# A frequency filter and a two-layer network: one product bank shared by two engines, later requests of x, four PSUM banks at first, and another queue for a split store

## The chip, the cores and the metric

The kernel runs on one core of a Trainium2 chip. The core has a matrix engine (TensorE, "PE" in the profile, with its weight loads as "PEld"), a vector engine (VectorE, "DVE"), an activation engine (ScalarE, "ACT"), GpSimd ("POOL") and SyncE ("SP"), which here only issues DMAs. Each engine works through its own instructions in order and waits on semaphores for the others. TensorE's results go to PSUM, which has eight banks of 512 floats per partition.

The metric is the device time of one execution in microseconds. The kernel before took 750.02 us (median of 14 runs, 749.25 to 751.09).

## The reference

```python
def _attn_ref(x, filt_r, filt_i):            # x: 8 x 3008 x 256
    X = np.fft.rfft(x, axis=1)
    F = (filt_r + 1j * filt_i)[None, :, :]
    return np.fft.irfft(X * F, n=x.shape[1], axis=1).astype(np.float32)

def _moe_ref(x, w_in, w_out):                # x: 24064 x 256, d_ff 2048
    h = x @ w_in
    g = np.maximum(0.01 * h, h)
    return (g @ w_out).astype(np.float32)
```

The output of the first is the input of the second; all inputs and the output are float32 in HBM.

## The kernel before

The Fourier transform over 3,008 points is split as 94 by 32. For each of the 8 batches there are four matmul stages: s1 (over 94 points), s2 (over 32), a product with the filter, sa (back over 32) and sb (back over 94), which leaves the mixed batch transposed in `yt`, in fp16. The network then takes the 24,064 rows in 47 chunks of 512: `moe1` multiplies `yt` by `w_in` into one of two double PSUM banks (`ph`, L505) and ScalarE applies the leaky ReLU into `gt_c` (L510); later chunks' second layer uses a seven-product scheme (L569), the first three chunks a plain one (L630).

All instructions are placed by hand or by a planner; each engine then runs its own list in that order.

**The first batch** is written out as a list of steps, the string `FIRST` (L461 to L478). Its five banks are b0 to b2 (single, `pf`) and b3, b4 (double, `ph`, 1,024 floats each). The steps that matter here:

- `s2p hf c n i b` fills bank b with stage s2 for n frequencies from c on, for channel half hf; i is 0 or 1 for the two terms of the complex product (L392, L396).
- `s2d` lets VectorE multiply such a bank by the filter into `prods` (L400). `s2a` lets ScalarE copy four frequencies of a bank to a spare in SBUF (L410), and `s2m` lets Pool multiply that spare by the filter (L400 too, on POOL).
- `sap hf c b` is stage sa for four frequencies (L420); it reads both products, i = 0 and 1. `sae` is ScalarE's copy of the result to `big2` (L423). `t2` is a VectorE transpose (L429); two of the four read channel half 0, two half 1. `sbp` is stage sb (L437) and `sbe` its copy to `yt` by ScalarE or VectorE (L336). `warm` are matmuls on idle data.
- `x 0`, `x 1` and `w_out` are DMA requests on Pool's queue: the two halves of the second batch's x (L191) and `w_out` (L456).

In `FIRST`, bank b4 holds s2 for half 1, frequencies 8 to 15, term 1 (`s2p 1 8 8 1 b4`); VectorE multiplies all of it (`s2d 1 8 8 1`). The bank is filled again by `s2p 1 0 8 0 b4`. On Pool the order is: six products, `x 0`, `s2m 1 16 8 0`, `s2m 1 16 8 1`, `x 1`, `w_out`.

**After the first batch** work is placed by planned times: `at(time, f)` puts f on a heap, and times are in units of which a chunk has `SL = 8`. The stages of the second batch (`s1_group`, L249 to L259, with their matmul at L254 and the copy at L257) run between the matmuls of the first chunks. Their banks come from `bank("pf", ...)` (L154), which goes round the list `single`. At the end of the first batch `single.pop()` (L489) leaves two banks in it; the third, `psp_last`, and `po_ps` become the output banks of the second layer, which uses them from time 8 on. `late_sb` (L446) places the rest of the first batch's stage sb among this work, from the same two banks.

**The stores.** A chunk's rows are stored in four blocks of 128 rows; `stores(ci, i)` issues blocks 2i and 2i + 1. A block that crosses a multiple of 376 rows is split into two requests. In the last chunk, i = 1 is stored first and i = 0 last, and block 1 (i = 0, j = 1) is a split one. All stores go out on SyncE's queue but for the last chunk's blocks with j = 1, which go out on ScalarE's (L584).

Of the kernel before, what the change touches and what calls it, by code (L numbers as in the profile page):

```python
# [75 lines left out]
def kernel(  # L76
# [9 lines left out]
    nc = tc.nc  # L86
    B, N, D = x.shape
# [6 lines left out]
    NCHUNK = TOK // CH  # L94
    assert NCHUNK * CH == TOK
    SL = 8
# [52 lines left out]
    single = [psp.tile([P, CH], FP32, name=f"pf{i}") for i in range(3)]  # L149
    po_ps = psp.tile([P, 2, D], FP32, name="po_ps")  # L150
    psp_last = single[-1]
# [12 lines left out]
    def at(time, f):  # L164
        clock["n"] += 1
        heapq.heappush(work, (time, clock["n"], f))
# [185 lines left out]
    act, dve = nc.scalar.copy, nc.vector.tensor_copy  # L352
# [6 lines left out]
    held, spare = {}, [scrp.tile([P, 4, DH], FP32, tag=f"p{i // 2 + 1}", name=f"spare{i}") for i in range(6)]  # L359
# [39 lines left out]
    def times_filter(eng, hf, c, n, i, x):  # L399
        eng.tensor_tensor(prods[hf][:, i, ds(c, n), :], x, fa_sb[:, ds(c, n), ts(hf, DH)], AL.mult)  # L400

    def s2d(hf, c, n, i):
        times_filter(nc.vector, hf, c, n, i, held.pop(("s2", hf, c, i)))

    def s2a(hf, c, n, i):

        at_c = c if ("s2", hf, c, i) in held else c - 4
        held["xf", hf, c, i] = xf = spare.pop(0)
        key = ("s2", hf, at_c, i)
        act(xf[:], (held.pop(key) if c - at_c == n - 4 else held[key])[:, ds(c - at_c, 4), :])  # L410

    def s2m(hf, c, n, i):
        xf = held.pop(("xf", hf, c, i))
# [44 lines left out]
    def round_x(n0, n, e):  # L458
# [10 lines left out]
        s2a 1 16 8 0, s2p 0 4 4 0 b1, s2p 1 16 8 1 b3, s2d 0 4 4 0, s2a 1 20 8 0, sap 0 8 b2, s2d 0 4 4 1,  # L469
        s2a 1 16 8 1, s2a 1 20 8 1, s2m 0 12 4 0, s2p 0 16 8 1 b4, sap 0 0 b1, s2p 1 0 8 1 b3, s2m 0 12 4 1,  # L470
        sap 0 12 b0, s2m 1 20 8 0, sae 0 8 A, s2d 0 16 8 1, sae 0 0 A, s2p 1 8 8 1 b4, sap 0 4 b2, s2d 1 0 8 1,
        sap 0 16 b1, sae 0 12 A, s2p 1 8 8 0 b3, sap 0 20 b0, s2d 1 8 8 1, s2m 1 20 8 1, sae 0 4 A,
        s2d 1 8 8 0, s2p 1 0 8 0 b4, sae 0 16 A, sap 1 20 b2, s2d 1 0 8 0, sap 1 12 b1, sae 0 20 A, sap 1 8 b0,
        x 0, s2m 1 16 8 0, sae 1 20 A, s2m 1 16 8 1, x 1, w_out, sae 1 12 A, sae 1 8 A, sap 1 16 b3,
        sae 1 16 A, sap 1 4 b2, t2 1, sae 1 4 A, sap 1 0 b4, t2 0, sae 1 0 A, warm 4, sbp 0 1 b1, sbp 0 4 b0,
        sbp 0 0 b3, sbp 0 3 b2, t2 3, sbe 0 1 A, sbe 0 4 A, sbe 0 0 A, sbp 0 2 b4, sbp 0 7 b1, sbp 0 6 b0,
        t2 2, sbe 0 2 A, sbe 0 7 A, sbp 0 5 b3, sbp 1 0 b4, sbp 1 1 b1, sbe 0 6 A, sbe 0 5 A, sbe 1 1 A,
        sbe 0 3 D, sbe 1 0 D  # L478
    """
    steps = dict(s1p=s1p, s1e=s1e, t1=t1, s2p=s2p, s2d=s2d, s2a=s2a, s2m=s2m, sap=sap, sae=sae, t2=t2,  # L480
                 sbp=sbp, sbe=sbe, x=load_x, w_out=load_w_out, xc=round_x, warm=keep_warm)
    for step in FIRST.split(","):
        what, *args = step.split()
# [5 lines left out]
    single.pop()  # L489
    out_banks = [t[:].rearrange("p (a t d) -> p a t d", a=2, t=2)  # L490
                 for t in (psp_last, po_ps.rearrange("p a d -> p (a d)"))]

    gts, osts, phs = {}, {}, {}

# [26 lines left out]
    s1, s2, s4 = (sums[:, i] for i in range(3))  # L521
# [26 lines left out]
    def store(ci, tj, of, queue=nc.sync):  # L548

        t, end = ci * CH + tj * P, ci * CH + (tj + 1) * P  # L550
        lo = 0
        while t < end:
            e = min(end, (t // QT + 1) * QT)
            b, h = divmod(t // QT, N2 // 4)
            row = b * N + (t % QT) // 4 * N2 + 4 * h
            queue.dma_start(
                bass.AP(tensor=out.tensor, offset=out.offset + row * D,
                        ap=[[N2 * D, (e - t) // 4], [D, 4], [1, D]]), of[lo : lo + e - t])
            lo, t = lo + e - t, e
# [15 lines left out]
    def rows(ci, i):  # L575

        if (ci, i) not in osts:
            osts[ci, i] = outp.tile([P, 2, 3, P], FP32, tag="ost", name=f"ost_c{ci}_h{i}")
        return osts[ci, i]

    def stores(ci, i, of=range(2)):
        for j in of:
            store(ci, 2 * i + j, rows(ci, i)[:, j, 0:2, :].rearrange("p k d -> p (k d)"),
                  nc.scalar if ci == NCHUNK - 1 and j else nc.sync)  # L584

    def twice(po):
        ap = [list(v) for v in po.ap]
# [4 lines left out]
    def last_product(ci):  # L592
        def after(po):
            add(rows(ci, 0)[:, :, 1], po, rows(ci, 1)[:, :, 2], AL.add)
            soon(AFTER[5], lambda: stores(ci, 0))
        return product(ci, lambda: sum_places(ci)[3], b22, after, 3)

    def products(ci):
        a11, a12, a21, a22 = (lambda i=i, j=j: quarter(ci, i, j) for i in range(2) for j in range(2))

        def after5(po):
            add(rows(ci, 1)[:, :, 1:3], twice(po), part[1], AL.add)
            soon(AFTER[5], lambda: stores(ci, 1))

        def m1():
            return product(ci, a11, b11, lambda po: nc.scalar.copy(t1, po))

        def m2():
            return product(ci, a12, b21, lambda po: add(rows(ci, 0)[:, :, 0], po, t1, AL.add))

        def m7():
            return product(ci, lambda: sum_places(ci)[1], wt[2], lambda po: add(v7, po, t1, AL.add), 1)

        if ci == NCHUNK - 1:
            items = last_product(ci - 1) + m1() + m7() + m2()
        elif ci > W0:
            items = m1() + last_product(ci - 1) + m2() + m7()
        else:
            done["products"] += 1
            items = m1() + [lambda: None] * (2 * NCH) + m2() + m7()  # L620
        items += product(ci, lambda: sum_places(ci)[2], wt[1], lambda po: add(part[1], twice(po), part[0], AL.add), 2)
        items += product(ci, a22, wt[3], lambda po: add(rows(ci, 1)[:, :, 0], po, u3, AL.add))
        items += product(ci, lambda: sum_places(ci)[0], wt[0], after5, 0)
        return items + last_product(ci) if ci == NCHUNK - 1 else items
# [44 lines left out]
    for b in range(1, B):  # L669
        z = 47 * (b - 4) if b > 4 else 0  # L670
        p = PLANS[min(b, 4) - 1]
# [18 lines left out]
    while queue:  # L690
        time, n, stage, b, g, f = heapq.heappop(queue)
# [62 lines left out]
```

## Time and profile before

| | |
|---|---|
| time, median of 14 runs | 750.02 us |
| the profiled execution, its time | 750.27 us |
| its span, first to last instruction | 748.5 us |
| ScalarE busy | 559.5 us, 75% |
| VectorE busy | 501.1 us, 67% |
| Pool busy | 164.1 us, 22% |
| first matmul of `moe1` (L505) | starts at 34.47 us |
| last vector result of the last chunk (L594) | starts at 742.84 us, takes 0.42 |

The span is what the trace covers; the execution's own time has 1.8 us around it. The profile's rows give start and length in us, the engine, the source line, and what the instruction writes and reads, then how many instructions are merged in the row; in brackets stands the idle time of the engine before it and the instruction that ended it. A queue that only issues DMAs has a q behind the engine's name. Matmuls overlap each other in the pipeline: a row of two matmuls of 0.38 us each that is 0.59 long has starts 0.21 apart. TensorE's granted clock is full in this run but for the last microseconds.

### The profile page before, as it was taken

How to read it: one execution, taken by the hardware profiler on the slowest of the kernel's cores; microseconds unless marked ns; L12 is line 12 of the kernel's file. 1: busy time of each engine (PE TensorE's matmuls, PEld its weight loads, DVE VectorE, ACT ScalarE, POOL GpSimd, SP SyncE). 2: the span in 40 equal slices, each digit the busy share in tenths (PEclk: the TensorE clock that was granted, in tenths of full speed). 3: DMA queues.
4: the chain of work that ended last, by engine and by line, in shares of the span. 5: the costliest groups of instructions: out<-in, count | busy, mean ns of one | idle time of the engine just before them, and what ended most of it. 6: DMA issues, size and time to landing. Idle time of an engine off the chain costs nothing.

```text
span 748.5 us, 19408 instructions
## 1 busy us (share of the span) xinstructions
PE 738.6 (99%) x8017; PEld 529.0 (71%) x8017; DVE 501.1 (67%) x684; ACT 559.5 (75%) x755; POOL 164.1 (22%) x171
## 2 busy tenths in 40 slices
PE   9999999999999999999999999999999999999996
PEld 3556667777687777877778777777777777777775
DVE  5987646766676765766777667766676675565565
ACT  4776797888778787777777787787777777777662
POOL 5603422332232212121232222121212210000000
PEclk9999999999999999999999999999999999999999
DMA  9997798887876666755675656544454333111111
GB/s 205 228 222 189 187 222 219 203 208 197 202 191 156 151 184 184 169 134 165 192 179 149 158 160 172 158 133 111 143 165 120 97 107 107 50 55 54 33 52 59
DMA packets 119560, 113.64 MB, mean 152 GB/s; under 512 B 16352, under 2 KB 92768, under 8 KB 119280
## 3 DMA queue, kind: packets, MB, share of 16 engines
q1 hardware_dynamic: 104127, 94.66, 42.7%
q0 software_dynamic: 15056, 17.49, 16.1%
q8 instruction: 62, 1.02, 0.6%
q10 hardware_dynamic: 289, 0.26, 0.1%
q14 instruction: 26, 0.21, 0.1%
HBM read 57.51 MB, written 50.33 MB: 144 GB/s over the span
## 4 chain that ended last, share of the span: by engine, by line
PE 93%; DMA 3%; DVE 2%; ACT 1%; issue 1%; POOL 0%; SPq 0%; DVEq 0%; POOLq 0%; ACTq 0%
PE ph L505 42%; PE po_ps L569 18%; PE pf L569 17%; PE pf L254 3%; PE pf L346 3%; PE pf L303 2%; PE pf L325 2%; DMA p_b_g<-p_b_g 2%; PE po_ps L368 1%; PE pf L630 1%; PE po_ps L630 1%; DMA dz<-big 1%; DMA big<-dz 0%; POOL y_b_g L318 0%; ACT yt L336 0%
## 5 line engine op out<-in xcount | busy, mean ns | idle before, releaser
L510 ACT ACTIVATE gt_c<-ph 128x1024 f16<-128x1024 f32 x376 | 385.6, 1026 | 134.8 <-PE ph L505 124.1
L505 PE MATMUL ph<-yt,w_in_sb 128*128 128x512 f16 (+7 forms) x1728 | 447.3, 351 | 0.2 <-ACT yt L336 0.2
L569 PEld LDWEIGHTS <-gt_c 128*128 128x128 f16 x2800 | 202.2, 98 | 91.2 <-issue 0.2
L318 POOL TENSOR_TENSOR y_b_g<-p_b_g,p_b_g 128x512 f16<-128x512 f32 x84 | 114.2, 1360 | 418.4 <-DMA p_b_g<-p_b_g 239.3
L569 PEld LDWEIGHTS <-big 128*128 128x128 f16 x2128 | 151.3, 98 | 61.6 <-issue 0.2
L505 PEld LDWEIGHTS <-w_in_sb 128*128 128x128 f16 x1728 | 137.5, 98 | 20.3 <-issue 0.7
L312 DVE TENSOR_TENSOR p_b_g<-pf,fb_sb 128x512 f32<-128x512 f32 x78 | 53.6, 688 | 32.4 <-PE pf L303 19.8
L569 PE MATMUL po_ps<-wt_sb,gt_c 128*128 128x128 f16 x704 | 70.0, 219 | 0.0
L569 PE MATMUL pf<-wt_sb,gt_c 128*128 128x128 f16 x688 | 68.4, 219 | 0.0
L569 PE MATMUL pf<-w_out_sb,gt_c 128*128 128x128 f16 x720 | 67.9, 219 | 0.0
L569 PE MATMUL po_ps<-wt_sb,big 128*128 128x128 f16 x720 | 67.4, 219 | 0.0
L569 PE MATMUL pf<-wt_sb,big 128*128 128x128 f16 x704 | 67.2, 219 | 0.0
L257 ACT CAST big<-pf 128x512 f16<-128x512 f32 x100 | 58.2, 587 | 11.9 <-PE pf L254 10.5
L569 PE MATMUL po_ps<-w_out_sb,gt_c 128*128 128x128 f16 x688 | 66.0, 219 | 0.0
L336 ACT CAST yt<-pf 128x376 f16<-128x376 f32 x120 | 56.4, 472 | 10.8 <-PE pf L346 7.9
L542 DVE TENSOR_TENSOR big<-gt_c 128x2048 f16<-128x2048 f16 (+1 forms) x46 | 57.9, 1259 | 0.1
L315 DVE TENSOR_TENSOR p_b_g<-pf,fa_sb 128x512 f32<-128x512 f32 x84 | 57.2, 681 | 0.2
L542 DVE TENSOR_TENSOR gt_c<-gt_c 128x2048 f16<-128x2048 f16 x43 | 55.4, 1288 | 1.0
L542 DVE TENSOR_TENSOR big<-gt_c,big 128x2048 f16<-128x2048 f16 (+1 forms) x45 | 55.2, 1227 | 0.0
L542 DVE TENSOR_TENSOR big<-big,gt_c 128x2048 f16<-128x2048 f16 (+1 forms) x45 | 54.6, 1212 | 0.1
L327 ACT CAST big<-pf 128x512 f16<-128x512 f32 x84 | 49.0, 584 | 4.9 <-PE pf L325 3.0
L254 PE MATMUL pf<-x_sb,small_sb 94*128 94x512 f16 x112 | 42.7, 381 | 0.6 <-ACT big L257 0.6
(88 smaller groups left out, 621.4 us busy)
## 6 DMA issues: line engine op xcount, KB each, us to landing
dz<-big SPq DMA_DIRECT2D x98, 256.0 KB
p_b_g<-p_b_g SPq DMA_DIRECT2D x156, 128.0 KB
out_dram<-ost_c_h SPq DMA_DIRECT2D x119, 128.0 KB
big<-dz SPq DMA_DIRECT2D x42, 256.0 KB
big<-dz SPq DMA_DIRECT2D x56, 192.0 KB
x_sb<-in_x_dram POOLq DMA_DIRECT2D x40, 192.0 KB, 4.8
x_sb<-in_x_dram POOLq DMA_DIRECT2D x2, 768.0 KB, 9.3
w_in_sb<-in_moe_w_in_dram POOLq DMA_DIRECT2D x1, 1024.0 KB, 13.5
```

Source lines behind the costliest of these rows:

```text
L254: nc.tensor.matmul(ps, fwd1[:N1], x_sb[:N1, ds(2 * g, 2), :], start=True, stop=True)
L257: copy(st[:, ds(2 * (g % 2), 2), :], ps)
L312: nc.vector.tensor_tensor(p2[:], ps, fb, AL.mult)
L315: nc.vector.tensor_tensor(p1[:], ps, fa, AL.mult)
L318: ("y", b, g), lambda: nc.gpsimd.tensor_tensor(y1[:], p1[:], p3[:], AL.add)))
L327: nc.scalar.copy(st2[h % 4][:, ds(2 * (g % 2), 2), :], ps)
L336: copy(yv, ps.rearrange("p c a -> p a c"))
L346: nc.tensor.matmul(ps[:, j, :], z2[h % 4][:K4, j, ts(dt, P)], i1_sb[:K4, 4 * h + j, :], start=True, stop=True)
L505: nc.tensor.matmul(ph[:, j, ds(t - ci * CH, e - t)], w_in_sb[:, dt, ts(ct, P)], yt[:, dt, ds(t % N, e - t)], start=(dt == 0), stop=(dt == ...
L510: nc.scalar.activation(gts[ci][:, ds(2 * g, 2), :], ph, AF.Lrelu)
L542: nc.vector.tensor_tensor(*(v[:, ds(c0, n)] for v in (o, i0, i1)), op)
L569: nc.tensor.matmul(po[:, t], a()[:, c, ts(t, P)], w[:, c, :], start=(c == 0), stop=(c == NCH - 1))
```

## The change

Four edits. In the first batch, bank b4's product for half 1, frequencies 8 to 15, term 1 is divided: ScalarE copies frequencies 8 to 11 (`s2a 1 8 8 1`), VectorE multiplies 12 to 15 out of PSUM (`s2h 1 12 8 1`), and Pool multiplies the copy (`s2m 1 8 8 1`), placed ahead of its two products for frequencies 16 to 19. The request `x 0` moves behind those two, next to `x 1`. After the first batch, `psp_last` and `po_ps` are added to the banks that `bank("pf", ...)` goes round, until time 7.6. In the last chunk, the store that goes out on ScalarE's queue for i = 0 is block 0 in place of block 1, so that SyncE issues the split block.

```diff
+    def four_of(hf, c, n, i):
+        at_c = c if ("s2", hf, c, i) in held else c - 4
+        key = ("s2", hf, at_c, i)
+        return (held.pop(key) if c - at_c == n - 4 else held[key])[:, ds(c - at_c, 4), :]
+
+    def s2h(hf, c, n, i):
+        times_filter(nc.vector, hf, c, 4, i, four_of(hf, c, n, i))
+
     def s2a(hf, c, n, i):
-        at_c = c if ("s2", hf, c, i) in held else c - 4
         held["xf", hf, c, i] = xf = spare.pop(0)
-        key = ("s2", hf, at_c, i)
-        act(xf[:], (held.pop(key) if c - at_c == n - 4 else held[key])[:, ds(c - at_c, 4), :])
+        act(xf[:], four_of(hf, c, n, i))
...
-        sap 0 16 b1, sae 0 12 A, s2p 1 8 8 0 b3, sap 0 20 b0, s2d 1 8 8 1, s2m 1 20 8 1, sae 0 4 A,
-        s2d 1 8 8 0, s2p 1 0 8 0 b4, sae 0 16 A, sap 1 20 b2, s2d 1 0 8 0, sap 1 12 b1, sae 0 20 A, sap 1 8 b0,
-        x 0, s2m 1 16 8 0, sae 1 20 A, s2m 1 16 8 1, x 1, w_out, sae 1 12 A, sae 1 8 A, sap 1 16 b3,
+        sap 0 16 b1, sae 0 12 A, s2p 1 8 8 0 b3, sap 0 20 b0, s2a 1 8 8 1, s2h 1 12 8 1, s2m 1 20 8 1,
+        s2m 1 8 8 1, sae 0 4 A, s2d 1 8 8 0, s2p 1 0 8 0 b4, sae 0 16 A, sap 1 20 b2, s2d 1 0 8 0, sap 1 12 b1,
+        sae 0 20 A, sap 1 8 b0, s2m 1 16 8 0, sae 1 20 A, s2m 1 16 8 1, x 0, x 1, w_out, sae 1 12 A, sae 1 8 A,
+        sap 1 16 b3,
...
     single.pop()
     out_banks = [t[:].rearrange("p (a t d) -> p a t d", a=2, t=2)
                  for t in (psp_last, po_ps.rearrange("p a d -> p (a d)"))]
+    single += [psp_last, po_ps.rearrange("p a d -> p (a d)")]
+    at(SL - 0.4, lambda: single.__delitem__(slice(2, 4)))
...
             store(ci, 2 * i + j, rows(ci, i)[:, j, 0:2, :].rearrange("p k d -> p (k d)"),
-                  nc.scalar if ci == NCHUNK - 1 and j else nc.sync)
+                  nc.scalar if ci == NCHUNK - 1 and i == j else nc.sync)
```

The order of the matmuls on TensorE is the same as before; only the banks that some of them write change.

More of the change, by code (lines that the diff above doesn't have):

```diff
@@ L471 @@
         sap 0 12 b0, s2m 1 20 8 0, sae 0 8 A, s2d 0 16 8 1, sae 0 0 A, s2p 1 8 8 1 b4, sap 0 4 b2, s2d 1 0 8 1,
-        sap 0 16 b1, sae 0 12 A, s2p 1 8 8 0 b3, sap 0 20 b0, s2d 1 8 8 1, s2m 1 20 8 1, sae 0 4 A,
-        s2d 1 8 8 0, s2p 1 0 8 0 b4, sae 0 16 A, sap 1 20 b2, s2d 1 0 8 0, sap 1 12 b1, sae 0 20 A, sap 1 8 b0,
-        x 0, s2m 1 16 8 0, sae 1 20 A, s2m 1 16 8 1, x 1, w_out, sae 1 12 A, sae 1 8 A, sap 1 16 b3,
[L475 to L478, printed above, removed]
+        sap 0 16 b1, sae 0 12 A, s2p 1 8 8 0 b3, sap 0 20 b0, s2a 1 8 8 1, s2h 1 12 8 1, s2m 1 20 8 1,
+        s2m 1 8 8 1, sae 0 4 A, s2d 1 8 8 0, s2p 1 0 8 0 b4, sae 0 16 A, sap 1 20 b2, s2d 1 0 8 0, sap 1 12 b1,
+        sae 0 20 A, sap 1 8 b0, s2m 1 16 8 0, sae 1 20 A, s2m 1 16 8 1, x 0, x 1, w_out, sae 1 12 A, sae 1 8 A,
+        sap 1 16 b3, sae 1 16 A, sap 1 4 b2, t2 1, sae 1 4 A, sap 1 0 b4, t2 0, sae 1 0 A, warm 4, sbp 0 1 b1,
+        sbp 0 4 b0, sbp 0 0 b3, sbp 0 3 b2, t2 3, sbe 0 1 A, sbe 0 4 A, sbe 0 0 A, sbp 0 2 b4, sbp 0 7 b1,
+        sbp 0 6 b0, t2 2, sbe 0 2 A, sbe 0 7 A, sbp 0 5 b3, sbp 1 0 b4, sbp 1 1 b1, sbe 0 6 A, sbe 0 5 A,
+        sbe 1 1 A, sbe 0 3 D, sbe 1 0 D
     """
-    steps = dict(s1p=s1p, s1e=s1e, t1=t1, s2p=s2p, s2d=s2d, s2a=s2a, s2m=s2m, sap=sap, sae=sae, t2=t2,
+    steps = dict(s1p=s1p, s1e=s1e, t1=t1, s2p=s2p, s2d=s2d, s2h=s2h, s2a=s2a, s2m=s2m, sap=sap, sae=sae, t2=t2,
                  sbp=sbp, sbe=sbe, x=load_x, w_out=load_w_out, xc=round_x, warm=keep_warm)
```

## The prediction

> **What bounds the kernel now.** I read the page's busy shares first, then the waits of TensorE alone after 34.9 us, then the chain of waits for the first batch, then short pieces of the timeline around each edited step, and last the stores at the end.
>
> ```profile
> PE 738.6 (99%) x8017; PEld 529.0 (71%) x8017; DVE 501.1 (67%) x684; ACT 559.5 (75%) x755; POOL 164.1 (22%) x171
> ...
> PE pf L303 <- DVE p_b_g L315: 1.0, 1, 1.0
> PE pf L254 <- ACT big L257: 0.6, 1, 0.6
> ...
> 26.02 0.47 PE ph L392 x8
> 26.51 0.92 DVE prod L400
> 27.44 0.22 issue
> 27.66 1.21 DVE prod L400
> 28.87 2.29 DVE big L429 x2
> ```
>
> TensorE is busy for 99% of the span. From 34.9 us to the end the view of waits lists for it only two waits, 1.0 and 0.6 us: apart from those the middle is a stream of matmuls, and an edit there can win at most a few tenths. So a gain or loss must come from the first 34.5 us, from the 0.6 us wait, or from the tail after the last matmul. Whatever the first stages win moves the whole stream, because nothing later holds TensorE against a fixed date; the 1.0 us wait (L303, at 66.50) stands at the end of a run of VectorE work that itself starts on TensorE's results (58.25 and 60.11), so it moves along and isn't filled.
>
> **The skill.** "PSUM — Partial Sum Buffer", section "PSUM bank collisions raise a hardware error", lets two engines read different banks at the same time; bank b4 (1,024 floats) is two of them. The order of the changed kernel's instructions does not use this: VectorE's new half product waits for a ScalarE semaphore at the value that the new copy sets, so the halves run one after the other. The same page, "The four PSUM rules", says Pool cannot reach PSUM, hence the copy; in this trace Pool's products all read a spare that ScalarE copied. "DMA: Bandwidth & Descriptors", section "Issuing engines are not separate DMA queues", says that issuing from several engines saves only issue time; the tail below agrees, since there issue time is what is late. Its section "SWDGE vs HWDGE vs iDMA" gives Pool one queue context; the landings of Pool's loads (30.1, 34.0, 37.4, 43.9 us) do come one behind another.
>
> **Part 1, the shared bank.** Removed: one VectorE product of 1,024 (1.21 us). Added: a ScalarE copy of 512 (0.59), a VectorE product of 512 (0.65) and a Pool product of 512 (two take 2.29, so one every 1.12).
>
> ```profile
> 24.99 0.60 POOL L191 DMA_DIRECT2D x_sb<-in_x_dram  x1
> 25.61 2.29 POOL L400 TENSOR_TENSOR prod<-spare,fa_sb 128x512 f16<-128x512 f32 x2
> 27.84 0.57 POOL L191 DMA_DIRECT2D x_sb<-in_x_dram  x1
> ...
> 28.67 0.59 PE L420 MATMUL ph<-prod,small_sb 128*128 128x512 f16 x2
> ...
> 30.43 0.66 ACT L423 CAST big<-ph 128x512 f16<-128x512 f32 x1
> ```
>
> VectorE looks like the bound (no idle from 14.6 to 33.9 us to speak of), but the chain says otherwise at one place: its product at 26.51 (s2d 1 8 8 0) follows TensorE's eight matmuls that start at 25.86, and TensorE is back to back up to there. The new order leaves these where they are. The bank b4 is filled at 25.05; the copy runs 25.13 to 25.72 (ScalarE is idle from 25.13 to 25.63), the half product 25.76 to 26.40, and VectorE then waits for 26.51 as before. **The 0.57 us that VectorE is spared turn into a wait for TensorE: gain 0.** The cover is thin: if the copy is over 0.1 us late, the product at 26.51 and the transposes at 28.87 slip with it.
>
> Pool is worse off. Its product at 23.88 ends at 25.05. The new one needs the copy: 25.80 to 26.93; then s2m 1 16 8 0 to 28.05 and s2m 1 16 8 1 to 29.2, where the latter ended at 27.90 although a request stood ahead of it. The second matmul of sap 1 16 (28.67 for the pair, 0.21 apart, so 28.89) waits for it: 29.27, 0.39 later. Behind it on TensorE stand sap 1 4, sap 1 0, four warming matmuls and sbp. The warming ones (29.96 to 30.83) lie before 31.20, when the second transpose releases sbp 0 1, so that start slips by only 0.1. ScalarE's last three copies (29.44, 29.93, 30.43) follow the matmuls: the last ends near 31.33 instead of 31.09, and the third transpose (31.13), which reads all of its half, starts 0.2 later. Transposes, sbp 1 0 and its VectorE copy then end 0.2 later, and so does the second matmul of L505 (34.84), which needs both halves of yt. **Cost 0.2**; at worst 0.5, if the thin cover fails as well; at best 0.6 won, if VectorE's spared time were the bound after all.
>
> **Part 2, the requests of x behind Pool's products.** The first half goes out near 29.2 instead of 24.99, the second near 29.8, w_out near 30.3 (28.40). Before, the first half landed 9.0 us after its request, at 33.96, but w_in was ahead in the same queue until 30.1, so 3.9 us were transfer. No row shows an idle queue for a load of this size; the nearest, the 192 KB load at 64.09, took 4.2. Bound from below: 29.2 plus the page's 1 us to a first byte (an estimate with "DMA: Bandwidth & Descriptors", "Specifications") plus 3.9, 34.1. From above: another 9.0, 38.2. I take 34.8, since w_in is out of the way by then. First use is L254 at 35.49 (35.7 with part 1): hidden, with 0.9 to spare. The second half lands 3.5 later (37.45 less 33.96), 38.3, for use past 41; w_out 6.4 later again (43.88 less 37.45), 44.7, for use at 45.6. **Cost 0.** The small loads of the third batch, behind them in the queue, are used only from 54.8 on.
>
> **Part 3, four banks at first.**
>
> ```profile
> 41.30 0.45 PE L437 MATMUL pf<-i_sb,big 128*64 128x94 f16 x8
> 41.68 0.58 ACT L257 CAST big<-pf 128x512 f16<-128x512 f32 x1
> 42.31 0.38 PE L254 MATMUL pf<-x_sb,small_sb 94*128 94x512 f16 x1 [0.56 <-ACT big L257]
> ```
>
> With two banks, group 8 (L254 at 42.31) takes the bank of group 7, which ScalarE empties only at 42.26, behind an activation (40.76 to 41.78). With four, it takes group 5's, emptied by VectorE at 40.29. After eight L437 matmuls the next kind starts 0.38 later elsewhere (47.50, then 47.88 for L630), so L254 can start at 41.68: 0.63 won. Next late are ScalarE's activations, which hold the two ph banks: moved up, they stand at most 0.05 behind TensorE's need at 43.6. The first product (45.99) now waits for group 10 to leave po_ps, but VectorE has that by 44.5, and for w_out, above. **Gain 0.6**, between 0.2 and 0.75.
>
> **Part 4, the split store.**
>
> ```profile
> 743.30 0.55 SPq L556 DMA_DIRECT2D out_dram<-ost_c_h  x1
> 743.46 1.20 ACTq L556 DMA_DIRECT2D out_dram<-ost_c_h  x1
> 744.71 0.93 ACTq L556 DMA_DIRECT2D out_dram<-ost_c_h  x1
> ...
> 736.11 1.54 SPq L556 DMA_DIRECT2D out_dram<-ost_c_h  x2
> ```
>
> The last block is ready at 743.26. ScalarE's queue issues its split half in two requests until 745.64; the program then ends 2.9 us later (748.5). SyncE's split pair at 736.11 took 1.54. On SyncE from 743.30 that gives 744.84, while ScalarE issues the whole half alone from 743.46, at most 1.2 long, until 744.66. **Gain 0.8**; the lower bound is 0.4, as SyncE's split pairs beside more traffic take up to 0.4 more (0.92 and 0.70 at 73.73), the upper 1.0.
>
> **Sum.** +0.2 + 0 - 0.6 - 0.8 = -1.2 us. The profiled execution took 750.27 us (span 748.5 and 1.8 around it), so 749.1 for it; it lies 0.25 over the median of the runs, 750.02, so 748.9 for the median, with 0.1 added for the thin covers.
>
> **Rivals.**
> - The first x half lands late and takes the place of the gains. One mechanism: a request costs its full 9.0 us whatever stands ahead, landing at 38.2; TensorE, in order, waits for it at the first L254. For: 8 to 9 us is what nearly all early Pool loads took. Against: they all queued behind one another, and the 192 KB one took 4.2. Price 38.2 - 35.7 = 2.5: -1.2 + 2.5 = +1.3, so 751.3, slower. It decides from a landing beyond 36.9, where the other gains are used up.
> - VectorE's spared time counts: Pool's delay turns out covered and the transposes start 0.6 earlier: -0.6 - 0.6 - 0.8 = -2.0, 748.0. Against it stand TensorE's matmuls of 25.86, which do not move.
> - The early gain is lost again, because ScalarE's activations become the bound once the bank wait goes, and the tail gives only its lower bound: +0.2 - 0.2 - 0.4 = -0.4, 749.6.
>
> **How the numbers follow.** Forecast 0.56, late x 0.14, spared time 0.14, lost gain 0.16. About 0.2% (1.5 us) is what a measurement tells from no change. Faster than 748.5: most of the spared-time case and a tenth of the forecast, 0.18. Slower than 751.5: under half of the late case, where the four banks are of no use either, and something not seen, 0.10. Within: 0.72. The forecast's own range is 748.3 to 749.7; with the rivals on either side 748.0 to 750.6.
>
> **What would show it.** After the change VectorE should show idle time of some 0.1 us before a product at 26.5, Pool's last product should end near 29.2 and the first L505 pair should run 0.2 later; L254 should follow the first late L437 at once; the second matmul stall, 1.0 us near 66, should remain, some 0.4 earlier; SyncE should have issued the last store by 744.9 and the span be near 747.3. I am wrong if TensorE waits at its first L254 for x, if the third transpose starts before 31.1, or if the last landing is again ScalarE's.

## The result

The changed kernel takes **753.89 us** (median of 10 runs, 751.34 to 754.87), the kernel before 750.27 us beside it (47 runs, 749.25 to 751.92). The ratio is 1.0044, 95% interval 1.0036 to 1.0051: slower by 0.44%, the whole interval above 1. The forecast of 748.9 and its range up to 750.6 are missed. The profiled execution took 754.66 us with a span of 752.9, which is 4.4 over the one before (748.5); between the medians it is 3.6.

### The profile page after: what moved, and what is told of

Its sections match the earlier page's. It is cut to its first block, busy times and chain, and to the rows that moved or that the text cites. A ratio compares the mean times of both kernels' runs of the same rounds, so it can differ in the third digit from the quotient of the medians.

```text
span 752.9 us, 19411 instructions
## 1 busy us (share of the span) xinstructions
PE 739.6 (98%) x8017; PEld 528.9 (70%) x8017; DVE 500.5 (66%) x684; ACT 560.0 (74%) x756; POOL 167.6 (22%) x172
## 4 chain that ended last, share of the span: by engine, by line
PE 91%; DMA 6%; POOL 1%; DVE 1%; issue 0%; ACT 0%; POOLq 0%; DVEq 0%; ACTq 0%
PE ph L516 41%; PE po_ps L580 18%; PE pf L580 18%; PE pf L254 3%; PE pf L346 3%; DMA w_out_sb<-in_moe_w_out_dram 3%; PE pf L303 2%; PE pf L325 2%; PE po_ps L641 1%; PE pf L641 1%; DMA x_sb<-in_x_dram 1%; DMA fa_sb<-in_filt_i_dram 1%; DMA dz<-big 1%; POOL prod L400 1%; DMA big<-dz 0%
## 5 line engine op out<-in xcount | busy, mean ns | idle before, releaser
L516 PE MATMUL ph<-yt,w_in_sb 128*128 128x512 f16 (+7 forms) x1728 | 447.8, 352 | 0.2
L318 POOL TENSOR_TENSOR y_b_g<-p_b_g,p_b_g 128x512 f16<-128x512 f32 x84 | 116.7, 1391 | 420.7 <-DMA p_b_g<-p_b_g 222.9
L516 PEld LDWEIGHTS <-w_in_sb 128*128 128x128 f16 x1728 | 137.6, 98 | 19.9 <-issue 0.6
L257 ACT CAST big<-pf 128x512 f16<-128x512 f32 x98 | 57.1, 588 | 11.9 <-PE pf L254 10.5
L254 PE MATMUL pf<-x_sb,small_sb 94*128 94x512 f16 x109 | 41.8, 383 | 0.0
```

What stands on the lines that cost most here:

```text
L254: nc.tensor.matmul(ps, fwd1[:N1], x_sb[:N1, ds(2 * g, 2), :], start=True, stop=True)
L257: copy(st[:, ds(2 * (g % 2), 2), :], ps)
L318: ("y", b, g), lambda: nc.gpsimd.tensor_tensor(y1[:], p1[:], p3[:], AL.add)))
L516: nc.tensor.matmul(ph[:, j, ds(t - ci * CH, e - t)], w_in_sb[:, dt, ts(ct, P)], yt[:, dt, ds(t % N, e - t)], start=(dt == 0), stop=(dt == ...
```

## The profile after

The view of waits of TensorE from 35 us to the end, in the changed kernel (what waited, for what, us in total, times, longest):

```profile
PE po_ps L641 <- DMA w_out_sb<-in_moe_w_out_dram: 4.1, 1, 4.1
PE pf L303 <- DVE p_b_g L315: 0.9, 1, 0.9
```

Before, these two places held the 1.0 us wait of L303 and the 0.6 us wait for a bank. The bank wait is gone, as it should be, and a wait that was not there before stands in its place: the first product of the second layer (L641, before L630) waits 4.1 us for `w_out`. (The diff moves line numbers: L400 and L191 stay, L254 too; L420, L423, L429, L437, L505 and L456 of before are now L427, L430, L436, L444, L516 and L463.)

The timeline of the changed kernel, cut to the pieces that answer to those shown of before:

```profile
23.74 5.64 POOL L400 TENSOR_TENSOR prod<-spare,fa_sb 128x512 f16<-128x512 f32 x5 [1.41 <-ACT big L430]
...
25.35 3.11 DVE L400 TENSOR_TENSOR prod<-ph,fa_sb 128x512 f16<-128x512 f32 x3 [0.42 <-ACT spare L417]
...
29.32 1.13 POOL L191 DMA_DIRECT2D x_sb<-in_x_dram  x2
29.43 0.38 PE L427 MATMUL ph<-prod,small_sb 128*128 128x512 f16 x1 [0.74 <-POOL prod L400]
...
30.43 1.18 POOL L463 DMA_DIRECT2D w_out_sb<-in_moe_w_out_dram  x1
...
31.47 2.37 DVE L436 STREAM_TRANSPOSE big<-big 128x1024 f32<-128x1024 f32 x2 [0.73 <-ACT big L430]
...
34.73 1.22 PE L516 MATMUL ph<-yt,w_in_sb 128*128 128x512 f16 x4
...
41.65 0.45 PE L444 MATMUL pf<-i_sb,big 128*64 128x94 f16 x8
...
42.03 0.39 PE L254 MATMUL pf<-x_sb,small_sb 94*128 94x512 f16 x1
...
45.30 0.60 PE L516 MATMUL ph<-yt,w_in_sb 128*128 128x512 f16 x2
...
50.03 1.03 PE L641 MATMUL po_ps<-w_out_sb,gt_c 128*128 128x256 f16 x4 [4.14 <-DMA w_out_sb<-in_moe_w_out_dram]
...
71.91 0.38 PE L303 MATMUL pf<-big,f_sb 128*128 128x256 f16 x2 [0.95 <-DVE p_b_g L315]
...
747.77 2.28 SPq L567 DMA_DIRECT2D out_dram<-ost_c_h  x3
747.94 0.42 DVE L605 TENSOR_TENSOR ost_c_h<-pf,ost_c_h 128x256 f32<-128x256 f32 x1 [0.20 <-PE pf L580]
```

The first product of the second layer and the stall at L303 before:

```profile
45.99 0.60 PE L630 MATMUL po_ps<-w_out_sb,gt_c 128*128 128x256 f16 x4
...
66.50 0.38 PE L303 MATMUL pf<-big,f_sb 128*128 128x256 f16 x2 [0.95 <-DVE p_b_g L315]
```

Read from the top of the first list. Pool's last five products now end at 29.38 and the requests follow at once: the two x halves from 29.32, w_out at 30.43. TensorE's `sap` waits 0.74 for Pool, the third transpose starts at 31.47 (31.13), the first pair of L516 at 34.73 (34.47). At 42.03 the L254 behind the late L444 starts 0.38 after it, without the wait for a bank. Then TensorE ends its work near 45.9 and stands until 50.03. At the end SyncE's three requests are issued by 747.77 + 2.28 = 750.05.

The 4.1 us are not the whole price. The same trace in windows (from:to, length, busy us and count of PE, PEld, DVE, ACT and POOL, granted TensorE clock, DMA share, GB/s):

```profile
50.00:51.00 1.00, 0.97 (x5) 0.71 (x6) 0.00 (x0) 0.00 (x0) 0.00 (x0) 0.50 1.01 264
...
53.00:54.00 1.00, 1.00 (x13) 0.69 (x14) 0.00 (x0) 1.00 (x2) 0.00 (x0) 0.98 1.15 346
```

Behind the wait the clock is 0.50 for some 3 us, until 53.03, although TensorE is busy: the same four products take 1.03 us for 0.60. From the first product to the stall at L303 it takes 71.91 - 50.03 = 21.88 us, where it took 66.50 - 45.99 = 20.51 before: 1.37 us more.

So, between the two profiled executions: at L303 the changed kernel is 71.91 - 66.50 = 5.41 us late. Of this 4.04 is the later first product (50.03 for 45.99, in which 0.3 lost at the start and 0.6 won at the bank are contained) and 1.37 the clock. From L303 to the end it wins 1.0 back: 0.7 in the tail (the span ends 4.9 us after the start of the last vector result, for 5.6 before) and 0.24 at a short stall near 197 us that is absent. Sum +4.4.

Why is `w_out` late? It was requested 2.03 us later (30.43 for 28.40) and landed 6.1 later (49.99 for 43.88). Two places in the DMA traffic differ. The first is what Pool's queue (q0) moved from 28 to 32 us; the columns are packets, MB and the time of the packets as a share of 16 engines. Before, then the changed kernel:

```profile
q0 software_dynamic: 135, 0.88, 105.9%
```

```profile
q0 software_dynamic: 51, 0.23, 43.2%
```

Nine tenths of w_in's packets have started by 27.8 us (its last ones start until 29.41), and in the changed kernel no request stands behind it yet. The queue lies nearly idle until the first packet of x at 30.62 and is at its full 0.2 MB per us again only from 32: it misses 0.65 MB, three microseconds of its rate. The second place is after 41 us, when SyncE's transfers for the second batch begin to move. The same view of the kernel before from 39 to 40 us, while w_out goes alone, and of the changed kernel from 43 to 44:

```profile
q0 software_dynamic: 386, 0.20, 144.8%
```

```profile
q0 software_dynamic: 212, 0.11, 78.2%
q1 hardware_dynamic: 206, 0.11, 51.5%
```

Both w_out and SyncE's writes to `dz` go in packets of 512 bytes here, and the queues get the same number of them (212 and 206): w_out's rate falls from 0.20 to 0.11 MB per us. Before, 100 of w_out's 2,048 packets (0.05 MB) were left at SyncE's first packet (41.04 us), in the changed kernel 1,211 (0.62 MB, at 41.45). This is the reading to be tested: **a queue that runs empty shifts a load into foreign traffic, where each byte costs it twice the time.**

## The experiments

In the table, "28 to 32" is what Pool's queue moved in that time, and the last columns are from the timed runs, each with the kernel before beside it (its median is 750.27 for the changed kernel, 750.13 for e1 to e4, 750.14 for e5 to e8, 749.98 for e9). The other columns are from one profiled execution of each.

| | first x request | 28 to 32, MB | 2nd x half landed | w_out landed | wait for w_out | us | ratio, 95% |
|---|---|---|---|---|---|---|---|
| before | 24.99 | 0.88 | 37.45 | 43.88 | 0 | 750.27 | |
| changed | 29.32 | 0.23 | 39.47 | 49.99 | 4.1 | 753.89 | 1.0044 (1.0036 to 1.0051) |
| e1_x_back | 25.16 | 0.85 | 37.93 | 44.13 | 0 | 748.87 | 0.9987 (0.9980 to 0.9993) |
| e2_x_only | 27.02 | 0.69 | 37.24 | 44.45 | 0 | 750.12 | 1.0002 (0.9993 to 1.0011) |
| e3_f2t_late | 29.16 | 0.29 | 39.46 | 47.79 | 2.0 | 753.18 | 1.0042 (1.0027 to 1.0057) |
| e4_banks_store | 26.08 | 0.84 | 37.42 | 44.33 | 0 | 748.82 | 0.9984 (0.9977 to 0.9991) |
| e5_wide_rows | 29.81 | 0.18 | 39.94 | 45.23 | 0 | 749.15 | 0.9986 (0.9980 to 0.9993) |
| e6_x_between | 27.35 | 0.62 | 37.64 | 44.33 | 0 | 749.62 | 0.9995 (0.9983 to 1.0008) |
| e7_warm | 28.77 | 0.33 | 39.43 | 47.47 | 0 (idle matmuls) | 753.98 | 1.0048 (1.0033 to 1.0063) |
| e8_no_share | 28.53 | 0.40 | 38.77 | 47.29 | 2.0 | 750.24 | 1.0008 (0.9988 to 1.0028) |
| e9_fill | 29.37 | 0.70 | 40.30 | 44.37 | 0 | 750.32 | 1.0009 (1.0000 to 1.0018) |

One more number bears on the reading, counted packet by packet: how much of w_out was still to be moved when SyncE's packets began. It is 0.04 to 0.10 MB in e1, e4 and the kernel before, 0.23 in e6 and 0.36 in e2, and w_out lands in time in all of these. It is 0.50 in e7, 0.51 in e8, 0.56 in e3 and 0.62 in the changed kernel, and in these it lands at 47.29 or later.

**e1_x_back**: the changed kernel with the first x request alone put back ahead of Pool's last three products.

```diff
-        sap 0 16 b1, sae 0 12 A, s2p 1 8 8 0 b3, sap 0 20 b0, s2a 1 8 8 1, s2h 1 12 8 1, s2m 1 20 8 1,
+        sap 0 16 b1, sae 0 12 A, s2p 1 8 8 0 b3, sap 0 20 b0, s2a 1 8 8 1, s2h 1 12 8 1, s2m 1 20 8 1, x 0,
...
-        sae 0 20 A, sap 1 8 b0, s2m 1 16 8 0, sae 1 20 A, s2m 1 16 8 1, x 0, x 1, w_out, sae 1 12 A, sae 1 8 A,
+        sae 0 20 A, sap 1 8 b0, s2m 1 16 8 0, sae 1 20 A, s2m 1 16 8 1, x 1, w_out, sae 1 12 A, sae 1 8 A,
```

> The changed kernel with the first x request back ahead of Pool's last three products; shared bank, four banks and store stay. Theory A (the late first request leaves Pool's queue empty near 29 us, everything behind it lands 2 us later, and w_out then runs into the second batch's traffic on SyncE's queue): first x half lands near 34, w_out before 45, no wait at the first L641, 749 to 749.5 us. Theory B (Pool's extra product is to blame, since it delays the w_out request by 2 us whatever x does): w_out still lands after 47, a wait of 2 us or more, 752 or above. Theory C (the four banks are to blame, as they bring the second batch's writes to DRAM forward): wait stays, 753 to 754.

Measured 748.87: the harm is gone and the three other parts bring 0.13%. w_out is still requested behind Pool's added product, at 29.81, 0.6 before the changed kernel, and lands 5.9 earlier. So that product and the four banks are not enough to make w_out late; the late place of the one request is needed as well.

**e2_x_only**: the kernel before with only this request moved behind Pool's last two products.

```diff
-        x 0, s2m 1 16 8 0, sae 1 20 A, s2m 1 16 8 1, x 1, w_out, ...
+        s2m 1 16 8 0, sae 1 20 A, s2m 1 16 8 1, x 0, x 1, w_out, ...
```

> The kernel before with the first x request moved behind Pool's two last products and nothing else. Pool has no extra product, so x goes out near 27.3 and w_out near 28.5, as before. Theory A in its plain form (the late x request alone is enough): w_out lands 2 us later and the wait appears, 752 or above. Theory B (it takes the extra product as well): x lands near 34, w_out near 44, no wait, 750.3 within 0.5.

Measured 750.12: no change. Without the added product the request goes out at 27.02, and the queue has only a short gap (0.69 MB).

**e3_f2t_late**: the changed kernel with SyncE's reload of 768 KB (`f2t`) issued later.

```diff
-    F2T = 3.24
+    F2T = 8.5
```

> The changed kernel with the 768 KB reload of the stage-two matrix (L678) requested at planned time 8.5 in place of 3.24, after w_out should have landed. If w_out's long transfer (10.5 us behind the second x half, against 6.4 before) comes from sharing the DMA engines with this reload, w_out lands near 46.5 and the wait at the first L641 falls from 4 us to 1 or less: 750 to 751. If it comes from the writes of the second batch to DRAM alone, or from Pool's own queue, the wait stays above 3 us: 753 to 754.

Measured 753.18 (four runs, 752.59 to 753.75), only 0.7 better. From 43 to 44 us the two queues move 209 and 211 packets, 0.11 MB each, as in the changed kernel, and the reload is requested only at 47.52. So the reload is not what holds w_out most of the time; the `dz` writes, which remain, are. In its profile the wait is 2.0 instead of 4.1 us, but this can't be put on the reload: in e7, below, which has the reload in its old place, w_out landed at 47.47, earlier than here. What the reload can add is seen in the changed kernel's profile: w_out's last six packets start 0.28 us apart from 47.64 to 49.05, about the length of one of the reload's 6 KB packets (0.23 to 0.25) and one of 512 bytes (0.06).

**e4_banks_store**: the kernel before with the four banks and the store's other queue only.

```diff
+    single += [psp_last, po_ps.rearrange("p a d -> p (a d)")]
+    at(SL - 0.4, lambda: single.__delitem__(slice(2, 4)))
...
-                  nc.scalar if ci == NCHUNK - 1 and j else nc.sync)
+                  nc.scalar if ci == NCHUNK - 1 and i == j else nc.sync)
```

> The kernel before with the four banks and the split store on SyncE, without the shared bank and with the requests of x as before. Theories A and B: both gains stand alone, 0.6 for the wait at 42 us and 0.7 at the tail: 749.0, ratio 0.9983. Theory C: the four banks bring on a wait for w_out: above 750.3.

Measured 748.82, 1.3 us better than the kernel before, where the prediction's two terms make 1.4. Against e1 (748.87), which has the shared bank besides, there is no difference that can be told: the shared bank is worth about nothing.

**e8_no_share**: e4 with the request moved as in e2, so parts 2, 3 and 4 without the shared bank.

```diff
-        x 0, s2m 1 16 8 0, sae 1 20 A, s2m 1 16 8 1, x 1, w_out, ...
+        s2m 1 16 8 0, sae 1 20 A, s2m 1 16 8 1, x 0, x 1, w_out, ...
```

> The kernel before with the later first x request, the four banks and the split store, but without the shared bank. Since Pool has no extra product the request goes out near 27, before its queue is empty: w_out in time, 748.5 to 749.0, the same as or a little below the run without the later request (748.82). If the later request is harmful as soon as the four banks bring the use of w_out forward: above 750.

Measured 750.24, from 748.54 to 755.91: the widest spread of all. Its profile has a wait for w_out (view of waits of TensorE up to 80 us):

```profile
PE po_ps L633 <- DMA w_out_sb<-in_moe_w_out_dram: 2.0, 1, 2.0
```

This was a surprise after e2, which has the same order on Pool. Pool's timeline suggests why. First e2, then e8:

```profile
22.55 4.53 POOL L400 TENSOR_TENSOR prod<-spare,fa_sb 128x512 f16<-128x512 f32 x4 [0.50 <-DMA fa_sb<-in_filt_i_dram]
```

```profile
24.05 4.53 POOL L400 TENSOR_TENSOR prod<-spare,fa_sb 128x512 f16<-128x512 f32 x4 [1.76 <-DMA fa_sb<-in_filt_i_dram]
```

Pool's four products start when the filter's load has landed, and this differs by 1.5 us between the two executions (22.4 and 23.9). A request behind the products inherits that: the first x half goes out at 27.02 in e2 and at 28.53 in e8. The old place inherits it too, but stands two products earlier: 24.99 before, with the filter at 22.61, and 26.08 in e4, with the filter at 23.68. And e4 and e8 are a clean pair: w_out is requested at 29.48 and 29.64, landing at 44.33 and 47.29. In this pair the time of its own request explains nothing; the bytes moved before do.

**e6_x_between**: the changed kernel with the first x request one product earlier.

```diff
-        ... s2m 1 16 8 0, sae 1 20 A, s2m 1 16 8 1, x 0, x 1, ...
+        ... s2m 1 16 8 0, x 0, sae 1 20 A, s2m 1 16 8 1, x 1, ...
```

> The changed kernel with the first x request between Pool's last two products, near 28.1 us, 1.1 earlier than in the change and 3 later than in the kernel before. If what counts is how long Pool's queue stands empty after w_in, the first half lands near 34.8, w_out near 46.5, and the wait at the first L641 is about 1 us or less: 749.5 to 751. If only the order behind both products counts (or the request's time does not), either 749 or 753.5.

Measured 749.62. Eleven of its twelve runs lie from 748.5 to 750.2 and one at 754.46, while the fastest run of the changed kernel took 751.34. So one product (1.1 us) is the distance between rare and nearly certain harm.

**e5_wide_rows**: the changed kernel with w_out loaded so that each partition takes 16 rows in succession, which makes packets of 8 KB. The second layer then multiplies the activations by other rows of w_out; the amount of work is the same.

```diff
-        nc.gpsimd.dma_start(w_out_sb[:], moe_w_out.rearrange("(ct p) d -> p ct d", p=P))
+        nc.gpsimd.dma_start(w_out_sb[:], moe_w_out.rearrange("(p ct) d -> p ct d", p=P))
```

> The changed kernel with w_out read as 16 consecutive rows per partition, so that each DMA packet holds 8 KB in place of 512 B; the second layer then multiplies by permuted rows of w_out. Theory A1 (from 41 us on the DMA engines take packets of w_out and of SyncE's 512 B writes one for one, so w_out's rate halves): with long packets w_out keeps nearly its full rate of 190 KB/us, lands near 45 although the first x half is still late, no wait at the first L641, 749 to 750. Theory A2 (the two queues share by bytes or time, whatever the packets are): w_out still lands at 48 or later, 752.5 to 754.

Measured 749.15. The requests and the x halves are as late as in the changed kernel, and the queue runs as empty (0.18 MB), yet w_out lands 5.3 us behind the second x half instead of 10.5. From 43 to 44 us:

```profile
q0 software_dynamic: 23, 0.19, 102.0%
q1 hardware_dynamic: 22, 0.01, 5.5%
```

Again the queues get equal numbers, 23 and 22, but w_out's packets are now sixteen times as long, and it keeps 0.19 MB per us. Long packets are not faster by themselves: from 40 to 41 us, alone, w_out moved 0.20 MB, as the short ones did before. When SyncE's packets began 0.45 MB of it were left, and it landed 3.5 us later; with 0.50 and 0.51 MB left in short packets it took 5.8 (e7) and 6.1 us (e8). The Trainium skill, "DMA: Bandwidth & Descriptors", section "Queues, rings and completion order", says that each DMA engine takes its queues in turn, one packet at a time; these two counts, and the 212 and 206 above, agree with it. The page has several descriptors in a typical packet; here the turns go by the single runs, of 512 bytes or 8 KB, that the profile lists. Of the two conditions of the harm, a queue that ran empty and packets as short as those of the other stream, this removes the second.

**e9_fill**: the changed kernel with w_out in two requests, the first half ahead of Pool's last products; the x requests keep their late place.

```diff
-    def load_w_out():
-        nc.gpsimd.dma_start(w_out_sb[:], moe_w_out.rearrange("(ct p) d -> p ct d", p=P))
+    def load_w_out(h):
+        cs = ds(int(h) * NCT // 2, NCT // 2)
+        nc.gpsimd.dma_start(w_out_sb[:, cs, :], moe_w_out.rearrange("(ct p) d -> p ct d", p=P)[:, cs, :])
...
-        ... s2a 1 8 8 1, s2h 1 12 8 1, s2m 1 20 8 1,
+        ... s2a 1 8 8 1, s2h 1 12 8 1, s2m 1 20 8 1, w_out 0,
...
-        ... s2m 1 16 8 1, x 0, x 1, w_out, sae 1 12 A, sae 1 8 A,
+        ... s2m 1 16 8 1, x 0, x 1, w_out 1, sae 1 12 A, sae 1 8 A,
```

> The changed kernel with w_out requested in two halves: the first 512 KB right behind s2m 1 20 8 1 (near 25 us, behind w_in in the same queue), the second 512 KB where w_out stood, behind x 0 and x 1, which keep their late place. Everything is computed; the one more request costs Pool about 0.6 us of issue time. Theory A (the queue that runs empty: after w_in the queue of Pool's loads has nothing to move from about 28 to 30.5 us, and the bytes it misses there are what is left of w_out when SyncE's small packets start): the queue never runs empty, the first half of w_out moves from 28 to 30.6, both x halves land at 36 or later as in the changed kernel, yet the last of w_out lands by 44.5, TensorE does not wait for it, time 748.7 to 749.5 (ratio 0.998 to 0.999). Theory D (what hurts is that x is requested late, by itself, whatever else the queue moves meanwhile): w_out, still behind x, comes late again and the time is 752 to 754.

Measured 750.32. This removes the first condition: in its profile the queue doesn't run empty, w_out lands at 44.37 although x comes later still, and the wait for it is gone. SyncE's packets begin later here, at 43.00, but at 41.45, where they began in the changed kernel, only 0.16 MB of w_out were left. The median is 0.8 us above the range that I expected. The profiled execution, the fastest of the twelve (749.62), shows two of the causes in the view of waits; what the slower ones add isn't seen:

```profile
PE ph L427 <- POOL prod L400: 0.7, 1, 0.7
PE pf L254 <- DMA x_sb<-in_x_dram: 0.7, 1, 0.7
```

The first x half now lands at 36.64 and the first L254 waits for it, the prediction's first rival at a quarter of its price (2.5), and the issue of one more request (25.06 to 26.01) delays Pool's added product, whose copy was ready at 25.19.

**e7_warm**: the changed kernel with 16 matmuls on idle data placed ahead of the first product of the second layer.

```diff
+    at(SL + 0.005, lambda: keep_warm(16))
```

> The changed kernel with 16 idle matmuls (3.5 us) put just ahead of the first second-layer matmul, that is, into the wait for w_out. Theory: the matmuls behind the wait run at half speed because TensorE stood idle for 4 us, which costs 1.4 us more. Then the wait stays, the clock stays at 1.00 behind it, and the time falls by 1 to 1.4: 752.3 to 753. Rival: the half speed has another cause (weights or DMA traffic at that moment): clock still 0.5 behind the wait, and the time as in the change or above, 753.5 to 754.5.

Measured 753.98, as slow as the changed kernel. Its timeline:

```profile
45.69 3.62 PE L368 MATMUL po_ps<-idle 128*128 128x512 f16 x16
...
49.14 0.60 PE L642 MATMUL po_ps<-w_out_sb,gt_c 128*128 128x256 f16 x4
```

The clock stays at 1.00 behind it, and from 49.14 to the stall at L303 (69.65) it takes 20.51 us, as in the kernel before: with the clock kept up, the 1.4 us behind the wait are gone. But w_out landed at 47.47 in this execution, and the idle matmuls hold the first product until 49.14. They pay 1.7 us to save at most 1.4.

## Why the prediction was wrong

**The step that failed** is in part 2: "w_out 6.4 later again (43.88 less 37.45), 44.7, for use at 45.6. Cost 0." The 6.4 us were the time of w_out's transfer in a trace where it had its queue and the DMA engines nearly to itself. They were carried over to a time 1 to 2 us later, at which SyncE's `dz` traffic is under way. Measured were 10.5 us behind the second x half (39.47 to 49.99). Of the 5.3 us by which w_out missed 44.7, 4.1 are this transfer and 1.2 the late x halves. The prediction looked for w_out's neighbours in Pool's queue only and named no cover for SyncE's, with 0.9 us to spare.

**A second term fed it.** For the first x half 34.8 was taken between 34.1 and 38.2; it was 35.80. The 3.9 us of transfer were a misreading: they were counted from the landing of w_in (30.11), but x's first packets had started at 27.72 already, so that its transfer took 6.2 us, beside the last of w_in. Behind an empty queue it took 5.2 (30.62 to 35.80), and the first packet came 1.3 us after the request. The 1.0 us passes on: 38.3 was forecast for the second half, 39.47 measured. The text had "w_in is out of the way by then" on the gain side. It is on the other side: with nothing behind w_in the queue misses 0.65 MB of transfer.

The rival of a late x did not come true in the changed kernel's profile, but by 0.04 us only: L254 starts at 35.84, unstalled, where the prediction saw 0.9 to spare. In e7, which is the same kernel up to there, x landed at 35.76 and L254 had to wait, since TensorE had come to it earlier:

```profile
PE pf L254 <- DMA x_sb<-in_x_dram: 0.4, 1, 0.4
```

The rival's own ground was misread as well: of the sixteen early Pool loads two took 8 to 9 us, the others 7.1 to 13.5.

**A third was not priced**: the clock at half behind a long wait, 1.4 us.

**What held.** Part 1, as e3 shows it, whose first batch is the changed kernel's and whose filter landed nearly as before (22.28; 22.61). Pool waits for ScalarE's copy, as forecast:

```profile
25.82 3.40 POOL L400 TENSOR_TENSOR prod<-spare,fa_sb 128x512 f16<-128x512 f32 x3 [0.94 <-ACT spare L417]
```

The forecast had 25.80 and an end at 29.2 (measured 29.23); the third transpose starts at 31.32 (0.19 later, 0.2 forecast) and the first L516 at 34.58, 0.11 later. In the changed kernel's own profile the likeness is luck: there the filter landed at 23.58, Pool started 0.16 us behind it (as in e2 and e8; the row names ScalarE) and ran its five products without a wait for the copy, and the end at 29.38 and the 0.26 at the first L516 come from that as well. From execution to execution the first L505 or L516 starts between 33.78 and 34.47 in the four profiles without the shared bank and between 34.18 and 35.23 in the seven with it, so that one pair says little. In the timed runs part 1 can't be told from zero (e1 against e4). Part 3: the L254 starts 0.38 behind the late L444, as forecast, for 1.01 before, 0.63 won. Part 4: 0.7 for the forecast 0.8. Parts 3 and 4 together made 1.3 us in e4 for the forecast 1.4. The sum without part 2 is then right, and e1, with everything but the late request, has 748.87, where 748.9 was forecast for the whole.

**Which of the edits is to blame** has no answer for one alone: the late request without the shared bank costs nothing in e2, and 1.4 us in the median of e8 (750.24 against e4's 748.82); the shared bank with the request in its old place costs nothing (e1). Together the added product and the move put the request 4.3 us later, when nearly all of w_in has been moved.

**The better version** is e1 or e4, which both beat the kernel before by 0.13 to 0.16%, with intervals below 1.

**What stays open**: why SyncE's first packet comes so long after its first `dz` request, 3.6 to 4.5 us in all eleven traces (37.34 and 41.04 before, 37.69 and 41.45 changed); why the filter's load lands at 22.2 to 23.9, differently from execution to execution; and why none of e2's twelve runs (749.15 to 751.35) is as late as e8's latest. The two ran on different chips, and only one execution of each was profiled, so that the filter's landing sets e8's spread is likely but not shown. How the harm is shared over the changed kernel's other runs (751.34 to 754.87) isn't shown either: one of them was profiled.

## What to carry to other kernels

Before a DMA request is moved, follow the whole queue behind it: a queue that runs empty pushes every later load, and each must be asked what else the DMA engines move at its new time, at what packet size. Here a load in packets of 512 bytes lost nearly half its rate (0.20 to 0.11 MB per us) to another stream of such packets; with rows of 8 KB it kept 0.19. A request that stands behind work whose start varies from run to run inherits the variation, so leave such slack as the worst start needs.

## What the runs showed of the hardware

- Two queues shared the DMA engines by counts of packets, not bytes: 512 against 512 bytes, 0.11 MB per us each; 8 KB against 512 bytes, 0.19 and 0.01.
- Where x was requested behind all or all but one of Pool's products, its first packet started 1.30 to 1.33 us after the request (eight traces). The 1 us that the prediction took for this was near. But in the changed kernel the queue was at its full rate only from 32, 2.7 us after the request at 29.32.
- TensorE's clock fell to half at waits of 2.0 us (e3 and e8) as at the one of 4.1. The Trainium skill, "TensorE: Matmul & The Clock Gate", section "Part 1: The HAM clock gate", names about 3.4 us of idle time; here 2.0 were enough. In e8 TensorE stood idle from 45.33 to 47.34, and was busy again when the clock fell, at 48.69, as the windows show:

```profile
47.00:48.00 1.00, 0.67 (x5) 0.51 (x6) 0.00 (x0) 0.00 (x0) 0.00 (x0) 1.00 1.07 299
48.00:49.00 1.00, 1.00 (x8) 0.43 (x8) 0.69 (x1) 0.30 (x1) 0.00 (x0) 0.84 1.06 337
49.00:50.00 1.00, 1.00 (x11) 0.58 (x11) 0.00 (x0) 1.00 (x2) 0.00 (x0) 0.50 0.99 337
```

  It stayed at half for 3.41 us, as in e3 and in the changed kernel, and cost 1.5 (from the first product to L303 21.99 us for 20.51), so a wait of 2 us was one of 3.5. The waits of 1.0 us at L303 left the clock at full.
